# Unused tiles of 64 and 192 bytes between the pools of a fused linear-attention and gated-MLP kernel

## The chip, the core and the metric

The kernel runs on one core of a Trainium2 chip. The core has five engines that matter here: PE (TensorE, matrix products), DVE (VectorE), ACT (ScalarE), POOL (GpSimd) and SP (which here only issues DMAs). In the profile, PEld is the loading of a matmul's stationary operand, PE the streaming of the moving operand through it. The metric is the device time of one execution in microseconds (us), lower being better: before the change the median of three runs is 1317.28 us (1316.2 to 1317.75).

## What is computed

Everything is float32. Linear attention over 8 batches, 8 heads, 576 positions and head size 64, then a gated MLP on 4608 tokens of width 512 with a hidden width of 1536:

```python
def phi(x):
    proj = np.einsum('bhsd,df->bhsf', x, w_phi)
    proj = proj - np.max(np.abs(proj), axis=-1, keepdims=True)
    return np.concatenate([np.exp(proj), np.exp(-proj)], axis=-1)
q_p, k_p = (phi(q), phi(k))
kv = np.einsum('bhsf,bhsd->bhfd', k_p, v)
z = np.sum(k_p, axis=2)
attn = einsum('bhsf,bhfd->bhsd', q_p, kv) / (einsum('bhsf,bhf->bhs', q_p, z)[..., None] + 1e-06)
x = attn.transpose(0, 2, 1, 3).reshape(4608, 512)
xn = x / sqrt(mean(x * x, axis=-1) + 1e-06) * rms_g
g, val = xn @ w_gate, xn @ w_val
return (g / (1 + exp(-g)) * val) @ w_out
```

## The kernel before

**Products in three matmuls.** Most operands are split into a high and a low part of the type fp32r (`_split`, L59 to L61: ACT copies the high part, DVE or POOL subtracts to get the low one). A product is then three matmuls, high by high, high by low, low by high, added up in PSUM. Each matmul has a stationary operand of 128 columns, loaded anew every time, and a moving operand of 65 to 512 columns.

**Stages.** The program has three stages, written one after the other, with some overlap.

*Attention with fill.* 32 pairs of heads go through a software pipeline (`front`, `mid`, `back`, `last`), in which the parts of several pairs are merged by hand-given due times. Between them stand pieces of two other kinds: weights arrive in 64-bit form and are decoded, and *fill* units compute the first 3 of the 12 columns of blocks (128 wide) of `w_gate` and `w_val` for 256 tokens at a time, as soon as their x is complete. `fill` (L468) splits x into the tile `xo` of the pool `a_xf` (two buffers) and each unit issues 12 matmuls (L482): the weight `fg` or `fv` is stationary, `xo` moves, 256 columns wide. ACT copies the result to `fo`, also of pool `a_xf`, six buffers (L485), and a DMA stores it. When the last pair is done, the units that are left run one after the other.

*Gate.* For nine blocks of 512 tokens the other 9 columns of blocks are computed (`gv`, L602). `parts` (L168) puts x's high and low part into the tile `xb` of pool `xo0` for even blocks and of pool `xo1` for odd ones. Each product has 12 matmuls at L614: the weight (`fg`, `fv`, or `wg`, `wv` of the pools `m_w0` to `m_w5`) is stationary, `xb` moves, 512 columns wide. A block has 18 such products, 216 matmuls. While it runs, the next block's x is fetched, normalised and split. Silu and product go to DRAM as `h`.

*Out.* For 18 groups of 256 tokens `h` is read back and multiplied by `w_out` by a Strassen-like scheme of 7 products (`omm`, L785). Each has 6 weight places `kp` (0 to 5) and three matmuls for each place, in the order high weight, low weight, high weight (L789 and L790): here the operand from x (`a11h` and its like) is stationary and the weight (`wh`, `wl`) moves, 256 columns wide. So a product has 18 matmuls and a group 126. Places 0 to 3 come from pool `rg`, which lies at the right end of the memory; places 4 and 5 from the pools `owp4` and `owp5` on the left.

```python
for i, (a, w) in enumerate(((xh, wh), (xh, wl), (xl, wh))):
    nc.tensor.matmul(place[n], a[:, kp], w[:, o], start=(first and kp == 0 and i == 0),
```

**Addresses.** A pool takes its bytes per partition off a stack when it is opened; the pools of one stage stand in the order in which they are opened, and a stage's stack lies over that of the stage before. Tiles begin at multiples of 32 bytes. In this layout the operands of the matmuls start at these bytes of each partition; the offsets of their slices are multiples of 512, so that the remainder mod 256 holds for each matmul of a row:

| stage | moving operand: bytes, mod 256 | stationary operand: bytes, mod 256 |
|---|---|---|
| projections (L319 to L321) | `wh`, `wl` 143392, 144416: 32 | `th`, `tl` 100832 to 106976: 224 |
| fill | `xo` 60192, 68384: 32 | `fg`, `fv` 21280 to 39712: 32 |
| gate, odd blocks | `xb` of `xo1` 68384: 32 | `fg`, `fv` and `wg`, `wv` 84768 to 148256: 32 |
| gate, even blocks | `xb` of `xo0` 101152: 32 | the same: 32 |
| out, places 0 to 3 | `wh`, `wl` 163808 to 213984: 224 | x's operands 52000 to 106272: 32 |
| out, places 4 and 5 | `wh`, `wl` 82720, 89888, 117536, 124704: 32 | the same: 32 |

**Who waits for bytes.** A pool that lands on bytes of released pools waits in one of two ways. With `reuse_waits="tile"` each tile waits only for the users of the earlier tiles on its own bytes; gate's and out's pools have this. Without it all tiles of the pool wait for every user of the pools that it lands on.

**Order.** Each engine executes its instructions in the order of the program; all large DMAs but those of x's 256-token loads and the gate weights stand in SP's queue.

Of the kernel before, what the change touches and what calls it, by code (L numbers as in the profile page):

```python
# [8 lines left out]
F32 = mybir.dt.float32  # L9
# [73 lines left out]
def kernel(ctx: ExitStack, tc: tile.TileContext, q, k, v, w_phi,  # L83
# [108 lines left out]
        waiting.update(i.name for i in nc.cur_bb.bb.instructions[n:])  # L192


    a_ctx = ExitStack()
    xfp = a_ctx.enter_context(tc.tile_pool(name="a_xf", bufs=2))
    ndp = a_ctx.enter_context(tc.tile_pool(name="a_nd", bufs=2))
    xips.append(a_ctx.enter_context(tc.tile_pool(name="a_xi", bufs=1)))
    wk = a_ctx.enter_context(tc.tile_pool(name="a_wk", bufs=2))
# [3 lines left out]
    dec = a_ctx.enter_context(tc.tile_pool(name="a_dec", bufs=1))  # L203
# [357 lines left out]
    g_ctx = ExitStack()  # L561
# [4 lines left out]
    def own(name, bufs=1):  # L566
        return g_ctx.enter_context(tc.tile_pool(name=name, bufs=bufs, reuse_waits="tile"))

    dec, xo1 = own("m_dec"), own("xo1")
    wps = {j: own(f"m_w{j}") for j in (4, 5)}  # L570
    xops = [own("xo0"), xo1]
    wps.update((j, own(f"m_w{j}")) for j in range(4))
    wk = own("m_wk", 2)
    pg_ctx = ExitStack()
# [123 lines left out]
    def left(name, bufs=1):  # L698
        return ctx.enter_context(tc.tile_pool(name=name, bufs=bufs, reuse_waits="tile"))

    ohp, stp, xof = left("ohp", 2), left("stp", 2), left("xof")
    owps = [left("owp4")]
    xol, osp = left("xol"), left("osp", 8)
    owps.append(left("owp5"))
    ow = left("ow", 3)
    opools = dict(a22=xol, s4=xol)
    ps_g = ctx.enter_context(tc.tile_pool(name="ps_g", bufs=2, reuse_waits="tile", space=PSUM))
# [66 lines left out]
    for gi in range(NG):  # L774
# [8 lines left out]
        ro = ow.tile([128, 5, DH], F32, name="ro")  # L783
# [78 lines left out]
```

## Time and profile before

| | |
|---|---|
| median of three runs | 1317.28 us |
| the profiled execution's own time | 1319.19 us |
| its span, first to last instruction | 1315.7 us |
| mean granted TensorE clock in it | 0.995 |
| instructions | 24224 |
| matmuls of gate (L614), of fill (L482), of out (L790) | 1944, 1296, 2268 |
| bytes moved by DMA | 197.12 MB |

The span is shorter than the execution by 3.5 us, the launch and the end. Busy times and starts are read from one profiled execution, in us from the start of the span. The ends of matmuls are modelled, so that two matmuls overlap in it; the interval from one start to the next is what tells the pace, and that is what is read below. The chain of work that ended last is followed back from the last instruction; where PE stands on it without a break, the pace of its matmuls is the pace of the kernel.

### The profile page before, as it was taken

The numbers are of one execution on the slowest core, as the hardware profiler recorded it, in microseconds if no ns is written. First come the engines' busy times: TensorE is split into PE (matmuls) and PEld (weight loads), VectorE is DVE, ScalarE is ACT, GpSimd is POOL, SyncE is SP. The second block draws the span as 40 slices with busy tenths as digits, with TensorE's granted clock in tenths as the row PEclk, the third lists the DMA queues.
The fourth block names the chain that finished last, engine by engine and source line by source line (L and its number), as shares of the span: only waits on it lengthen the run. The fifth ranks groups of instructions, "written<-read, shape, count | busy, mean of one in ns | idle before, by whom it ended". The sixth has DMA issues, their size and how long they took to land.

```text
span 1315.7 us, 24224 instructions
## 1 busy us (share of the span) xinstructions
PE 1279.0 (97%) x8886; PEld 1190.3 (90%) x8886; DVE 839.8 (64%) x1228; ACT 705.3 (54%) x1472; POOL 623.7 (47%) x580
## 2 busy tenths in 40 slices
PE   7989999999999999899999999999999999999998
PEld 7989989999999898899888888888888899999998
DVE  7889887787788962311245645644545786788773
ACT  6878787787778874534233433432332444444442
POOL 4666665565555854201323223323211277776773
PEclk9999999999999999999999999999999999999999
DMA  5445575666656437444536435434425544445441
GB/s 163 127 128 149 163 183 144 156 182 170 172 160 177 126 102 214 159 153 138 170 102 210 144 130 198 145 126 162 139 87 165 185 142 148 144 131 164 143 141 48
DMA packets 198228, 197.12 MB, mean 150 GB/s; under 512 B 69024, under 2 KB 154912, under 8 KB 198112
## 3 DMA queue, kind: packets, MB, share of 16 engines
q1 hardware_dynamic: 179104, 181.44, 45.1%
q10 hardware_dynamic: 19008, 14.16, 4.0%
q8 instruction: 70, 1.15, 0.4%
q14 instruction: 46, 0.38, 0.1%
HBM read 126.04 MB, written 69.50 MB: 149 GB/s over the span
## 4 chain that ended last, share of the span: by engine, by line
PE 85%; DVE 5%; DMA 5%; ACT 2%; issue 1%; SPq 1%; POOL 0%; ACTq 0%; POOLq 0%; DVEq 0%
PE gp L614 18%; PE gq L614 15%; PE gd L790 6%; PE gy L790 6%; PE gz L790 6%; PE sm L482 6%; PE acc L359 6%; PE fp L482 5%; PE sm L423 4%; PE fp L790 3%; PE fp L423 2%; PE pp L321 2%; PE pp L319 2%; PE pp L320 2%; PE sm L372 2%; PE sm L306 2%
## 5 line engine op out<-in xcount | busy, mean ns | idle before, releaser
L388 POOL TENSOR_TENSOR ql<-eq,qh 128x256 fp32r<-128x256 f32 x256 | 216.8, 879 | 58.6 <-issue 31.7
L599 DVE TENSOR_TENSOR h<-sl,gp 128x512 f32<-128x512 f32 x81 | 55.5, 685 | 167.4 <-PE gp L614 153.5
L614 PE MATMUL gp<-xb,wv 128*128 128x512 f32 x648 | 158.4, 389 | 0.0
L614 PEld LDWEIGHTS gp<-xb,wv 128*128 128x128 f32 x648 | 121.2, 188 | 24.7
L614 PE MATMUL gq<-xb,wg 128*128 128x512 f32 x576 | 138.3, 389 | 0.0
L54 POOL TENSOR_TENSOR wa<-raw,wa 128x192 f32<-128x192 f32 (+1 forms) x112 | 66.8, 618 | 140.2 <-DVE wa L52 46.1
L359 PE MATMUL acc<-vm,ek 128*128 128x65 f32 x1024 | 131.0, 270 | 0.0
L614 PEld LDWEIGHTS gq<-xb,wg 128*128 128x128 f32 x576 | 108.1, 188 | 22.4
L359 PEld LDWEIGHTS acc<-vm,ek 128*128 128x128 f32 x1024 | 127.4, 194 | 0.5 <-ACT ek L346 0.4
L323 DVE TENSOR_REDUCE mx<-pp 128x4 f32<-128x512 f32 (+1 forms) x160 | 100.9, 631 | 30.4 <-PE pp L321 29.0
L384 ACT ACTIVATE qh<-sm 128x512 fp32r<-128x512 f32 (+1 forms) x192 | 97.4, 508 | 0.0
L597 ACT ACTIVATE sl<-gq 128x512 f32<-128x512 f32 x72 | 42.7, 593 | 97.0 <-PE gq L614 94.7
L319 PE MATMUL pp<-wh,th 128*128 128x256 f32 x288 | 88.6, 309 | 4.7 <-ACT th L60 1.5
L61 POOL TENSOR_TENSOR xb<-x,xb 128x1024 fp32r<-128x1024 f32 x18 | 46.3, 2594 | 97.9 <-ACT xb L60 97.9
L383 ACT ACTIVATE eq<-sm 128x512 f32<-128x512 f32 x128 | 78.5, 613 | 14.2 <-PE sm L372 11.1
L321 PE MATMUL pp<-wh,tl 128*128 128x256 f32 x288 | 84.4, 299 | 0.2 <-DVE tl L61 0.2
L320 PE MATMUL pp<-wl,th 128*128 128x256 f32 x288 | 81.2, 283 | 0.0
L614 PE MATMUL gp<-xb,fv 128*128 128x512 f32 x324 | 77.8, 389 | 0.0
L346 ACT ACTIVATE ek<-yk 128x512 f32<-128x512 f32 x128 | 75.3, 649 | 1.1 <-DVE yk L326 1.1
L154 POOL TENSOR_TENSOR ss<-ss,sq 128x512 f32<-128x512 f32 x27 | 34.9, 1291 | 80.9 <-ACT sq L153 80.9
L614 PEld LDWEIGHTS gp<-xb,fv 128*128 128x128 f32 x324 | 60.8, 188 | 12.6
L614 PE MATMUL gq<-xb,fg 128*128 128x512 f32 x288 | 69.2, 389 | 0.0
(210 smaller groups left out, 3803.4 us busy)
## 6 DMA issues: line engine op xcount, KB each, us to landing
hs<-h SPq DMA_DIRECT2D x108, 256.0 KB
ht<-hs SPq DMA_DIRECT2D x18, 1536.0 KB
gvs<-fo SPq DMA_DIRECT2D x108, 128.0 KB
gvr<-gvs SPq DMA_DIRECT2D x27, 512.0 KB
rc<-di SPq DMA_DIRECT2D x32, 288.0 KB
x<-xs ACTq DMA_DIRECT2D x18, 512.0 KB
x<-xs SPq DMA_DIRECT2D x9, 1024.0 KB
kt<-in_k_dram SPq DMA_DIRECT2D x32, 256.0 KB
```

The costliest lines, as they stand in the source:

```text
L319: nc.tensor.matmul(o, th[:, cs], wh, start=True, stop=False)
L320: nc.tensor.matmul(o, th[:, cs], wl, start=False, stop=False)
L321: nc.tensor.matmul(o, tl[:, cs], wh, start=False, stop=True)
L323: nc.vector.tensor_reduce(mx[:, 0:2 * m], pp[:, 0:2 * m], axis=AX.X, op=ALU.max, apply_absolute_value=True)
L359: nc.tensor.matmul(acc[:, sg, h], e[h][:, sg, j], vm[:, h, j], start=False, stop=(h == 1 and j == T0 - 1))
L383: nc.scalar.activation(ei[:, sg], yi, AF.Exp, scale=1.0 - 2.0 * sg)
L384: nc.scalar.activation(hi[:, sg], yi, AF.Exp, scale=1.0 - 2.0 * sg)
L388: nc.gpsimd.tensor_tensor(lo[:, sg, cs], ei[:, sg, cs], hi[:, sg, cs].bitcast(F32), ALU.subtract)
L423: nc.tensor.matmul(o[:, 0:SH], a[:, h, sg], e[:, sg, h, cs], start=(i == 0), stop=(i == 5))
L482: nc.tensor.matmul(fp[:, 0:TF], w, xx[x][:, c], start=(i == 0), stop=(i == 3 * NC - 1))
L614: nc.tensor.matmul(gp[:, 0:T], w, e[:, c], start=(i == 0), stop=(i == 3 * NC - 1))
L790: nc.tensor.matmul(place[n], a[:, kp], w[:, o], start=(first and kp == 0 and i == 0), stop=(kp == KP - 1 and i == 2), skip_group_check=True)
```

## The change

The change adds a function that opens a pool with one tile of n bytes per partition, which nothing writes or reads, and calls it ten times. In the attention stage it stands ahead of the pool of `xo` and `fo` (192 bytes) and behind it (64). In gate it stands around `xo1` (192 ahead, 64 behind) and around `xo0` (64 ahead, 192 behind). In out it stands around `owp4` and around `owp5` (192 ahead, 64 behind each). No instruction of the program is added, removed or moved by it in the source; the new pools are opened without `reuse_waits`.

```diff
+    def pad(c, at, n):
+        c.enter_context(tc.tile_pool(name=f"pad{at}", bufs=1)).tile([128, n // 4], F32, name=f"pad{at}")
+
     a_ctx = ExitStack()
+    pad(a_ctx, "x", 192)
     xfp = a_ctx.enter_context(tc.tile_pool(name="a_xf", bufs=2))
+    pad(a_ctx, "n", 64)
     ndp = a_ctx.enter_context(tc.tile_pool(name="a_nd", bufs=2))
...
-    dec, xo1 = own("m_dec"), own("xo1")
+    dec = own("m_dec")
+    pad(g_ctx, "xo1", 192)
+    xo1 = own("xo1")
+    pad(g_ctx, "w4", 64)
     wps = {j: own(f"m_w{j}") for j in (4, 5)}
+    pad(g_ctx, "xo0", 64)
     xops = [own("xo0"), xo1]
+    pad(g_ctx, "w0", 192)
     wps.update((j, own(f"m_w{j}")) for j in range(4))
...
     ohp, stp, xof = left("ohp", 2), left("stp", 2), left("xof")
+    pad(ctx, "ow4", 192)
     owps = [left("owp4")]
+    pad(ctx, "xol", 64)
     xol, osp = left("xol"), left("osp", 8)
+    pad(ctx, "ow5", 192)
     owps.append(left("owp5"))
+    pad(ctx, "ro", 64)
     ow = left("ow", 3)
```

Added up along each stack, the remainders become these; all other operands keep theirs, since each pair of tiles adds up to 256 bytes:

| operand | mod 256 before | after | moving less stationary, before | after |
|---|---|---|---|---|
| `xo` (fill, moving), and `fo` | 32 | 224 | 0 | 192 |
| `xb` of `xo1` (gate, odd blocks, moving) | 32 | 224 | 0 | 192 |
| `xb` of `xo0` (gate, even blocks, moving) | 32 | 96 | 0 | 64 |
| `wh`, `wl` of `owp4` and `owp5` (out, moving) | 32 | 224 | 0 | 192 |

## The prediction

> **What bounds the kernel now.** First the page's busy times, then the windows (each engine's busy time in a stretch; the first column of numbers is the stretch's length), then the chain of waits, then single instructions.
>
> ```profile
> PE 1279.0 (97%) x8886; PEld 1190.3 (90%) x8886; DVE 839.8 (64%) x1228; ACT 705.3 (54%) x1472; POOL 623.7 (47%) x580
> PE 85%; DVE 5%; DMA 5%; ACT 2%; issue 1%; SPq 1%; POOL 0%; ACTq 0%; POOLq 0%; DVEq 0%
> ```
> ```profile
> 200.00:300.00 100.00, 96.97 (x806) 95.61 (x805) 80.78 (x146) 80.57 (x202) 59.28 (x74) 0.98 0.60 165
> 300.00:400.00 100.00, 99.80 (x850) 99.41 (x849) 80.15 (x138) 76.85 (x196) 55.29 (x68) 1.00 0.59 161
> 500.00:554.00 54.00, 47.30 (x299) 42.63 (x298) 14.51 (x17) 22.05 (x44) 17.93 (x13) 0.97 0.63 195
> 554.00:630.00 76.00, 76.00 (x614) 74.97 (x613) 14.87 (x20) 30.66 (x73) 8.74 (x7) 1.00 0.45 144
> 680.00:730.00 50.00, 50.00 (x222) 41.44 (x221) 26.57 (x40) 19.28 (x33) 14.69 (x16) 1.00 0.49 163
> 1100.00:1200.00 100.00, 100.00 (x868) 100.00 (x867) 74.58 (x68) 42.03 (x55) 77.20 (x35) 1.00 0.48 146
> ```
>
> PE is the bound: from 554 us on it never stops, while DVE, ACT and POOL have room. Up to 500 us it is at 95 to 99%; only from 500 to 554 us it stops for 6.7 us. So what counts is the interval between the starts of two matmuls. The chain gives it (start, length, what, number):
>
> ```profile
> 579.87 8.62 PE sm L482 x72
> ...
> 772.16 2.72 PE gp L614 x12
> ...
> 1051.28 4.17 PE gy L790 x36
> ...
> 1065.84 2.20 PE gy L790 x19
> ```
>
> Gate: 2.72 us for 12, 226.7 ns each, 512 columns wide. Fill: 8.62 us for 72, 119.7 ns, 256 wide. A column thus costs (226.7 - 119.7) / 256 = 0.418 ns, 107 ns for 256 and 214 ns for 512, and both kinds pay some 13 ns for each matmul on top, whatever its width. Out: a group takes 1065.84 - 1051.28 = 14.56 us for 126, 115.6 ns each, also 256 wide: 4 ns less than fill, for a matmul of one form. The timeline of out says where that comes from (start, length, line, names):
>
> ```profile
> 1065.68 0.28 PE L790 MATMUL gy<-wh,a12h 128*128 128x256 f32 x1
> ...
> 1066.03 0.28 PE L790 MATMUL gy<-wh,a12h 128*128 128x256 f32 x1
> ...
> 1067.05 0.28 PE L790 MATMUL gy<-wh,a12h 128*128 128x256 f32 x1
> ...
> 1067.76 0.28 PE L790 MATMUL gy<-wh,s2h 128*128 128x256 f32 x1
> ```
>
> These are the starts of weight places 0, 1 and 4, and of the next product. Places 1 to 3 take (1067.05 - 1066.03) / 9 = 113.3 ns each, 6 above the columns; places 4 and 5 take 0.71 / 6 = 118.3 ns; place 0, the first after 4 and 5 of the product before, takes 0.35 / 3 = 116.7 ns. Line, width, type and stationary operand are the same; what differs is the weight's place in memory, 224 mod 256 against an operand at 32 for places 0 to 3, and 32 against 32 for 4 and 5. Fill and gate have 32 against 32 throughout, and pay the 13 ns throughout. This pair of paces is the heart of the forecast: equal remainders cost some 7 ns for each matmul, a distance of 192 does not.
>
> A third distance occurs in the projections, moving `wh` at 32, stationary `th` at 224, so a distance of 64 (of 256):
>
> ```profile
> 279.90 0.28 PE L319 MATMUL pp<-wh,th 128*128 128x256 f32 x1
> ...
> 280.84 0.28 PE L321 MATMUL pp<-wh,tl 128*128 128x256 f32 x1
> ```
> ```profile
> 25.76 0.28 PE L319 MATMUL pp<-wh,th 128*128 128x256 f32 x1
> ...
> 27.01 0.28 PE L321 MATMUL pp<-wh,tl 128*128 128x256 f32 x1
> ```
>
> The first row of matmuls has nine, (280.84 - 279.90) / 8 = 117.5 ns, so 10.5 ns above the columns; the second has twelve, 1.25 / 11 = 113.6 ns. The distance of 64 has two paces, then, and I see no more than which instructions stand around it.
>
> **The change part by part.** The tiles issue nothing, so the whole effect is the pace at new addresses.
>
> *Out.* Places 4 and 5 go from distance 0 to 192, as places 1 to 3 have it. At 113.3 ns for all, a group takes 14.28 us instead of 14.56, 0.28 us less, times 18 groups: 5.0 us. I take **4.9**. All rows are of this line itself; the cover is that nothing else is due within it. The nearest to it is the loop of `ht`: DVE's first work on a group waits for its load, and the next load is issued behind that work.
>
> ```profile
> 1107.36 1.59 DVE L726 TENSOR_TENSOR st<-ht 128x768 f32<-128x768 f32 x1 [3.35 <-DMA ht<-hs]
> ```
> ```profile
> 1120.81 0.96 DVE L726 TENSOR_TENSOR st<-ht 128x768 f32<-128x768 f32 x1 [2.23 <-DMA ht<-hs]
> ```
>
> It turned once in 13.45 us here, 0.8 us under the new 14.28. If it were the bound, the group could not go below it, and the change would still get its 0.28 us.
>
> *Fill.* The windows of L482 alone (busy time of PE and PEld, with counts):
>
> ```profile
> 450.00:500.00 50.00, 21.55 (x160) 20.06 (x161) 1.00 0.35 104
> 500.00:554.00 54.00, 28.60 (x214) 27.50 (x212) 0.97 0.63 195
> 554.00:630.00 76.00, 71.72 (x588) 71.53 (x588) 1.00 0.45 144
> ```
>
> Distance 0 becomes 192, at the same width as in out: 119.7 to 113.3 ns, 6.4 ns. From 554 us on, 588 matmuls give **3.8** us, since PE never stops there. The other 708 of the 1296 would give 4.5 us if PE set the end all the time; at 95 to 99% busy with chains of small DMAs between (DMA has 5% of the chain) I take 60%, **2.7** us, with 0 and 4.5 as ends. The `fo` tiles shift with `xo`: their stores move the same bytes, and DMA is at 0.45 of its time from 554 us on; cost nothing, and with six buffers ACT would have to be late by units of 1.4 us before PE saw it.
>
> *Gate, odd blocks.* Distance 0 to 192, 4 blocks of 216 matmuls. No row shows 512 columns at another distance than 0. The ends: nothing, if the 13 ns of this width are no matter of addresses, and all 13 ns (11.2 us), if no cost were left. I take the row of out, 113.3 against 119.7 ns and the same 13 ns on top of the columns in gate and in fill: 6.4 ns, 864 x 6.4 = **5.5** us.
>
> *Gate, even blocks.* Distance 64, 5 x 216 = 1080 matmuls. By the nine matmuls of the projections (10.5 ns instead of 13) it is 2.5 ns, 2.7 us; by the twelve 6.4 ns, 6.9 us; nothing is the lower end. I take the nine, **2.6** us, because they stand in the steady part of the attention stage and the twelve at its first pairs. Nothing else becomes due: the next block's x is ready early.
>
> ```profile
> 739.35 4.83 POOL L61 TENSOR_TENSOR xb<-x,xb 128x1024 fp32r<-128x1024 f32 x2 [12.86 <-ACT xb L60]
> ```
> ```profile
> 1048.99 0.28 PE L790 MATMUL fp<-wh,a11h 128*128 128x256 f32 x1
> ```
>
> POOL has the parts of a block ready at 744.2 us. Out's first matmul starts at 1048.99; a block is 216 matmuls and, but for the last, two more of the same width for the next block's norm, 49.4 us, the last 49.0. Counted back from 1048.99, a block begins at 1048.99 - 49.0 - 5 x 49.4 = 753 us: 8.8 us of room, against some 1.4 us by which a block becomes shorter.
>
> Sum: 4.9 + 3.8 + 2.7 + 5.5 + 2.6 = 19.5 us. The profiled execution took 1319.2 us, so 1299.7; on the median of the runs shown, 1317.3, it makes **1297.8**.
>
> **The rivals.**
>
> *B, the distance of 64 is as good as 192.* For it: the twelve at 113.6 ns; gate is one long stream of one kind, and the pace of a stream seems to settle into one of two. Against it: the nine, also a stream, stay at 117.5. Time: 1080 x 3.9 ns = 4.2 us more, **1293.6**.
>
> *C, the 512-wide matmuls do not follow.* Their 13 ns could belong to the width or to what follows a matmul; all rows of gate have one pace, whatever the weight, so no row speaks for addresses there. Against it: the same 13 ns in fill, on another width. Then 8.1 us are lost: **1305.9**.
>
> *D, the addresses do nothing.* The difference between places could come from where the pools lie at large (places 0 to 3 lie above 163808, the others below 131872). Against it: the weights of gate are spread from 21280 to 150304 and show one pace. Then the time stays at **1317**. The Trainium skill's page "SBUF — State Buffer", section "Who interferes with whom", speaks for this case: it gives TensorE two read ports, one for the moving operand and one for the weight load, calls them independent, and has it that PE never waits on anyone. By that rule a load and a stream could not meet at any address. The trace disagrees in the 5 ns between the places of out.
>
> *E, slower: the new pools make the gate stage wait.* They are opened without `reuse_waits="tile"`, on bytes of the attention stage. If the wait for all users went over to what lies beside them, no gate unit could start before the last fill unit, at 630 us. Of L614 alone:
>
> ```profile
> 500.00:554.00 54.00, 19.86 (x83) 15.32 (x84) 0.97 0.63 195
> ```
>
> These 83 matmuls (83 x 226.7 ns = 18.8 us) fill gaps now and would come on top, and with them the first weights' way to PE, among it x's own split (4.83 us on POOL in the row above): some 24 us against 19.5 gained, **1322**. It decides as soon as the wait costs more than 19.5 us. Against it: nothing reads or writes the new tiles, so nothing of theirs could wait.
>
> **How the numbers follow.** The forecast, with 117.5 ns at the distance of 64, has 0.46, B 0.32, C 0.12, D 0.06, E 0.04. The forecast's own range, with 0 to 4.5 us from the fill units before 554 us, is 1296 to 1300.5, B's 1292 to 1296.5; a gate that loses all 13 ns on odd blocks would reach 1288. These two cases hold 0.78, so the range goes on to C: 1289 to 1306. Differences under 0.2% (2.6 us) can't be told from none by a measurement of this kernel. Forecast, B and C are faster by more than that, 0.90 together; D is the same, 0.06; E is slower, 0.04.
>
> **What would show it.** In the chain and timeline after: out's places 4 and 5 at 113.3 ns, and place 0 too, a group in 14.28 us; fill's 72 matmuls in 8.16 us instead of 8.62; gate's 12 matmuls in 2.64 us for odd blocks, and for even ones 2.69 (forecast) or 2.64 (B); 2.72 in both is C. With all three at their old pace it is D. L614 with no matmul before the last of L482 is E. The forecast is wrong, too, if PE begins to show idle time after 554 us, in out first behind the load of `ht`.

## The result, and the profile after

The changed kernel is slower. Its median over 10 runs is 1325.16 us (1319.94 to 1328.27); the kernel before, run beside it, has 1314.72 us over 10 runs (1311.03 to 1317.75). The ratio is 1.0075, with a 95% interval of 1.0056 to 1.0094. The forecast was 1297.8 us and the range ended at 1306. The profiled execution took 1327.44 us, its span is 1324.4 us.

First the page of the kernel after: the busy times, and the chain's share of each engine.

```profile
PE 1285.8 (97%) x8886; PEld 1188.9 (90%) x8886; DVE 843.5 (64%) x1228; ACT 704.9 (53%) x1472; POOL 624.8 (47%) x580
...
PE 81%; DVE 8%; DMA 4%; ACT 3%; issue 2%; SPq 1%; POOL 1%; ACTq 0%; POOLq 0%; DVEq 0%
```

The counts are those of before and PE is busy 6.8 us longer. The windows show that it still never stops from 554 us on (length of the stretch, then busy time and count of PE, PEld, DVE, ACT and POOL):

```profile
554.00:630.00 76.00, 76.00 (x617) 74.21 (x616) 14.47 (x22) 30.88 (x73) 10.27 (x8) 1.00 0.48 151
...
1100.00:1200.00 100.00, 100.00 (x851) 100.00 (x850) 75.07 (x68) 41.51 (x55) 73.57 (x35) 1.00 0.49 148
```

The two lines point in opposite directions: 617 matmuls where there were 614 in the first stretch, 851 where there were 868 in the second. No wait was added; the pace itself changed, for the better in one stage and for the worse in another. The chain of waits of the kernel after gives the paces (start, length, what, how many):

```profile
567.85 8.48 PE sm L487 x72
...
576.80 8.17 PE sm L487 x72
...
625.38 24.73 PE gp L624 x108
...
790.58 2.80 PE gq L624 x12
...
812.77 2.75 PE gq L624 x12
...
1054.97 4.24 PE gy L804 x36
...
1069.81 4.24 PE gy L804 x36
...
1307.25 4.24 PE gy L804 x36
```

- Fill (L487): 8.48 / 72 = 117.8 ns in one row, 8.17 / 72 = 113.5 ns in the next. Before it was 119.7. So fill gains, but one row keeps a worse pace than the next at the same addresses.
- Gate (L624): odd blocks 2.80 / 12 = 233.3 ns, even blocks 2.75 / 12 = 229.2 ns. Before, both took 226.7. Gate loses in every block.
- Out (L804): a group takes 1069.81 - 1054.97 = 14.84 us instead of 14.56.

For the sums of the stages two more rows of the chain of before are needed, the start of gate and the last row of the first product:

```profile
629.79 24.51 PE gp L614 x108
...
1298.80 4.16 PE gy L790 x36
```

| stretch | before | after | difference |
|---|---|---|---|
| up to the start of gate's long row | 629.79 | 625.38 | -4.4 |
| from there to the first whole `gy` row of out | 421.49 | 429.59 | +8.1 |
| 17 groups of out | 247.52 | 252.28 | +4.8 |

Together +8.5 us, of the 8.7 us by which the spans differ. In out the single matmuls show what happened to the pair of paces that was the heart of the forecast; these are again places 0, 1 and 4 and the next product, in the timeline of the kernel after:

```profile
1069.65 0.28 PE L804 MATMUL gy<-wh,a12h 128*128 128x256 f32 x1
...
1070.00 0.28 PE L804 MATMUL gy<-wh,a12h 128*128 128x256 f32 x1
...
1071.06 0.28 PE L804 MATMUL gy<-wh,a12h 128*128 128x256 f32 x1
...
1071.77 0.28 PE L804 MATMUL gy<-wh,s2h 128*128 128x256 f32 x1
```

Places 1 to 3 take 1.06 / 9 = 117.8 ns, places 4 and 5 take 0.71 / 6 = 118.3 ns, the same within the 10 ns to which the rows are given. The moved places did not come to 113.3. The places that nobody moved left it: same tiles, same addresses as before, and 4.5 ns more for each matmul. So a matmul's pace isn't a property of its own two addresses alone.

### The profile page after: what moved, and what is told of

Same layout as the page of the kernel before. It is cut to its first block, busy times and chain, and to the rows that moved or that the text cites. A ratio compares the mean times of both kernels' runs of the same rounds, so it can differ in the third digit from the quotient of the medians.

```text
span 1324.4 us, 24224 instructions
## 1 busy us (share of the span) xinstructions
PE 1285.8 (97%) x8886; PEld 1188.9 (90%) x8886; DVE 843.5 (64%) x1228; ACT 704.9 (53%) x1472; POOL 624.8 (47%) x580
## 4 chain that ended last, share of the span: by engine, by line
PE 81%; DVE 8%; DMA 4%; ACT 3%; issue 2%; SPq 1%; POOL 1%; ACTq 0%; POOLq 0%; DVEq 0%
PE gp L624 18%; PE gq L624 15%; PE gd L804 6%; PE gz L804 6%; PE gy L804 6%; PE sm L487 5%; PE acc L364 5%; PE fp L487 4%; PE sm L428 4%; PE fp L804 3%; PE pp L326 2%; PE fp L428 2%; PE pp L324 2%; PE pp L325 2%; DVE mx L328 1%
## 5 line engine op out<-in xcount | busy, mean ns | idle before, releaser
L624 PE MATMUL gp<-xb,wv 128*128 128x512 f32 x648 | 161.2, 394 | 0.0
L624 PEld LDWEIGHTS gp<-xb,wv 128*128 128x128 f32 x648 | 121.2, 188 | 27.4 <-ACT sl L607 0.2
L624 PE MATMUL gq<-xb,wg 128*128 128x512 f32 x576 | 140.9, 393 | 0.0
L624 PEld LDWEIGHTS gq<-xb,wg 128*128 128x128 f32 x576 | 108.2, 188 | 25.0
L624 PE MATMUL gp<-xb,fv 128*128 128x512 f32 x324 | 79.2, 393 | 0.0
L624 PEld LDWEIGHTS gp<-xb,fv 128*128 128x128 f32 x324 | 60.9, 188 | 13.9
L624 PE MATMUL gq<-xb,fg 128*128 128x512 f32 x288 | 70.5, 393 | 0.0
```

The source lines that it names most:

```text
L624: nc.tensor.matmul(gp[:, 0:T], w, e[:, c], start=(i == 0), stop=(i == 3 * NC - 1))
```

## The experiments

Two questions stood open after the result. Why did out's unmoved places lose 113.3 ns? And do 512-wide matmuls follow the same rule as 256-wide ones? The theories: **L**, that a row of matmuls at distance 192 (moving less stationary, mod 256) has two steady paces, some 113.3 and 117.8 ns, and keeps the one that its beginning leads it into; and its rivals, that it is the **alignment** of the two starts within 64 bytes that counts, not their distance; that out took over its pace from the changed **gate**; and that each place keeps its own pace, so that the loss came from somewhere else.

**A map of paces.** This kernel computes nothing of the reference. It runs rows of 30 fp32r matmuls on constant data, 256 or 512 wide, with the stationary operand at 32 or at 0 mod 256 and the moving one at ten distances, behind none, one or two short matmuls.

```diff
+SETS = [(256, 32, [0, 16, 32, 64, 96, 128, 160, 192, 224, 240]), (256, 0, [...]), (512, 32, [...]), (512, 0, [...])]
+            nc.tensor.matmul(p[:, 0:width], wt[:, s0 + (i % 12) * 128:s0 + (i % 12 + 1) * 128],
+                             xt[:, m0 + (i // 3 % 4) * width:m0 + (i // 3 % 4 + 1) * width], start=(i == 0), stop=(i == n - 1))
```

> This kernel computes nothing of the reference: it runs streams of 30 fp32r matmuls on constant data, 256 and 512 columns wide, with the stationary operand at 32 or 0 mod 256 and the moving one at a distance of 0, 16, 32, 64, 96, 128, 160, 192, 224 or 240 bytes from it, each three times, behind nothing, one or two short matmuls. Theory P (each pair of remainders has one pace): each distance has one interval in all three streams, about 113 ns (256 wide) at 64 and 192, about 120 at 0. Theory L (a stream at another distance than 0 has two steady paces and keeps the one into which its beginning leads it): at 64 and 192 some streams of 256 columns hold 113.3 ns and others 117.7 from their first ten matmuls to the end, at 0 all hold 120; at 512 columns 0 gives 226.7 and the others 229 or 233, or a faster pace near 220. Theory A (the 6.7 ns that remain at 113.3 come from starting at 32 within 64 bytes): the streams with both operands at a multiple of 64 are faster than 113.3 and 220 ns.

The timeline shows each row of 30 in one line. The name of its tile holds width, remainder of the stationary operand, distance and the number of short matmuls ahead (p256s32d64r0). From the start of one row to that of the next is the time of 30 matmuls:

```profile
21.59 3.56 PE L110 MATMUL p256s32d64r0x<-xt,wt 128*128 128x256 f32 x30
24.99 3.76 PE L110 MATMUL p256s32d96r0x<-xt,wt 128*128 128x256 f32 x30
28.59 3.73 PE L110 MATMUL p256s32d128r0x<-xt,wt 128*128 128x256 f32 x30
...
442.26 7.00 PE L110 MATMUL p512s0d0r0x<-xt,wt 128*128 128x512 f32 x30
449.10 7.11 PE L110 MATMUL p512s0d16r0x<-xt,wt 128*128 128x512 f32 x30
```

At 256 wide, distance 64 takes (24.99 - 21.59) / 30 = 113.3 ns and 96 takes 3.60 / 30 = 120.0 ns. At 512 wide, distance 0 takes 6.84 / 30 = 228.0 ns, with the beginning of the row in it. Taking the last 18 intervals of each row alone, and both remainders of the stationary operand:

| distance | 256 wide, ns | 512 wide, ns |
|---|---|---|
| 0 | 120.0 | 226.7 |
| 64 | 113.3 in one row, 117.8 in the two behind short matmuls | 228.9 |
| 192 | 113.3; with the stationary at 0: 113.3 once, 117.8 twice | 233.3 |
| 96 | 120.0 | 233.3 |
| 16 to 240, the others | 116.4 to 120.0 | 231.3 to 236.7 |

Three things follow. At 256 wide distance 0 is among the worst, as the forecast had it. At 512 wide it is the best. And at 64 and 192 the same row of matmuls can have 113.3 or 117.8 ns, depending on what went ahead. Alignment falls: with the stationary operand at 0 or at 32 the values are the same but for which of two paces is met. Nor are 64 and 192 alone in this: 240 has 233.3 or 236.7 ns at 512 wide, 16 has 116.7 or 118.7 ns at 256 wide, by what went ahead.

The map also answers what the forecast took for granted. 226.7 ns is twice 113.3: at the best pace of each width a column costs 0.443 ns, and no fixed cost for each matmul shows on top. The 13 ns that the forecast found on top of the columns came of comparing the best pace at 512 with one of the worst at 256.

**Out alone.** Only the four tiles around `owp4` and `owp5`.

```diff
+    pad(ctx, "ow4", 192)
     owps = [left("owp4")]
+    pad(ctx, "xol", 64)
...
+    pad(ctx, "ow5", 192)
     owps.append(left("owp5"))
+    pad(ctx, "ro", 64)
```

> Only the four unused tiles of the out stage are left, fill and gate stand as before. Theory P: places 0 to 5 all at 113.3 ns, a group of 126 in 14.28 us instead of 14.56, some 5 us faster. Theory L: without the matmuls at distance 0 in places 4 and 5, which lead the stream back to 113.3 ns in each product, the whole stage holds one pace, as in the changed kernel 117.7 ns: a group in 14.84 us, 5 us slower. If the pace of out in the changed kernel was carried over from its gate stage, out is at 113.3 here and the kernel 5 us faster.

It took 1322.34 us over 6 runs beside 1316.08 for the kernel before, ratio 1.0042 (1.0021 to 1.0063). Its chain:

```profile
588.04 8.62 PE sm L485 x72
...
1050.36 4.24 PE gy L797 x36
1065.19 4.24 PE gy L797 x36
```

Fill keeps its old 8.62 us for 72. The group takes 14.83 us, as in the full change, and all six places stand between 117.7 and 118.0 ns. Gate is untouched here, so the worse pace isn't carried over from gate: taking the three matmuls of each of places 4 and 5 away from distance 0 is enough to lock the whole stage at 117.8 ns.

**Fill alone.** Only the 192 bytes ahead of `a_xf` and the 64 behind.

```diff
+    pad(a_ctx, "x", 192)
     xfp = a_ctx.enter_context(tc.tile_pool(name="a_xf", bufs=2))
+    pad(a_ctx, "n", 64)
```

> Only the two unused tiles around the pool of x's parts in fill are left, gate and out stand as before. Both theories expect a gain from fill alone. Theory P: all 72 matmuls of a block at 113.3 ns, 8.16 us instead of 8.62, some 6 us faster in all. Theory L: some streams at 113.3 and some at 117.7 ns, 8.16 or 8.48 us, some 4 us faster, with gate at 2.72 us for 12 and out at 14.56 for a group as before.

1310.40 us over 4 runs, ratio 0.9955 (0.9938 to 0.9973): this part is a gain. Its chain:

```profile
571.92 8.48 PE sm L487 x72
...
1042.46 4.17 PE gy L795 x36
1057.02 4.16 PE gy L795 x36
```

Out's group stays at 14.56 us. Five rows of 72 in the stage's end all take 8.48 us, 117.8 ns: here fill met only the worse of the two paces, and still gained 1.9 ns on 119.7.

**A finer map.** The same rows at 32 distances in steps of 8, two rows each, stationary at 32; it too computes nothing of the reference.

```diff
-SETS = [(256, 32, [0, 16, 32, 64, ...
+SETS = [(512, 32, [0, 8, 16, 24, ..., 248]), (256, 32, [0, 8, 16, 24, ..., 248])]
```

> As the first map (nothing of the reference is computed), with the distance in steps of 8 bytes from 0 to 248, 512 and 256 columns, two streams each. Theory M (the steady pace is a function of width and distance, with two steady paces at 64 and 192 for 256 columns): the values of the first map come again at its distances, 226.7 ns at 0, 228.9 at 64 and 233.3 at 192 for 512 columns, and no distance between is under 226.7. A rival: there is a distance at which 512 columns run near 220 ns, which the coarse map stepped over; then gate could be made faster by shifting x's parts there.

```profile
11.55 6.99 PE L110 MATMUL p512s32d0r0x<-xt,wt 128*128 128x512 f32 x30
18.38 7.17 PE L110 MATMUL p512s32d8r0x<-xt,wt 128*128 128x512 f32 x30
...
179.04 7.16 PE L110 MATMUL p512s32d192r0x<-xt,wt 128*128 128x512 f32 x30
186.04 7.14 PE L110 MATMUL p512s32d200r0x<-xt,wt 128*128 128x512 f32 x30
...
490.79 3.69 PE L110 MATMUL p256s32d64r0x<-xt,wt 128*128 128x256 f32 x30
494.32 3.75 PE L110 MATMUL p256s32d72r0x<-xt,wt 128*128 128x256 f32 x30
...
512.31 3.61 PE L110 MATMUL p256s32d112r0x<-xt,wt 128*128 128x256 f32 x30
515.76 3.81 PE L110 MATMUL p256s32d120r0x<-xt,wt 128*128 128x256 f32 x30
```

512 wide: 6.83 us at distance 0, 7.00 us at 192; in the last 18 intervals 226.7 ns at 0 is the lowest of all 32, 228.9 at 64 the next, the highest 236.7. 256 wide: distance 64 now takes 3.53 / 30 = 117.7 ns behind a row at 56, where the first map had 113.3 for the same pair of addresses behind a row at 32. That is theory L in one pair of lines. Distance 112 came to 113.3 ns both times, and 120 is the worst with 122.2.

**Gate alone.** Only the four tiles around `xo1` and `xo0`.

```diff
+    pad(g_ctx, "xo1", 192)
+    xo1 = own("xo1")
+    pad(g_ctx, "w4", 64)
     wps = {j: own(f"m_w{j}") for j in (4, 5)}
+    pad(g_ctx, "xo0", 64)
     xops = [own("xo0"), xo1]
+    pad(g_ctx, "w0", 192)
```

> Only the four unused tiles around xo1 and xo0 in gate are left. Theory M: 12 matmuls take 2.80 us in odd blocks (192) and 2.75 in even ones (64), as the first map has it for 512 columns, against 2.72: 864 x 6.7 + 1080 x 2.2 ns = 8 us slower, and fill and out as before. Theory P, on which the prediction was built: 2.64 us in odd blocks, 5 us faster or more.

1324.69 us over 9 runs beside 1316.45, ratio 1.0059 (1.0032 to 1.0087).

```profile
668.09 2.80 PE gq L622 x12
...
718.72 2.75 PE gq L622 x12
...
763.28 2.80 PE gq L622 x12
```

The blocks alternate at 233.3 and 229.2 ns, the values of the maps at distances 192 and 64. From the last fill matmul to out's first it is 428.0 us, 8.5 more than the 419.5 before. By the maps one expects 864 x 6.6 ns + 1080 x 2.2 ns = 8.1 us. The three parts alone make +6.3, -5.7 and +8.2 us, together +8.8; the whole change made +10.4.

**Fill with place 4 alone, fill with place 5 alone.** If the three matmuls at distance 0 are what leads the others back to 113.3 ns, one place left at 0 must do.

```diff
+    pad(a_ctx, "x", 192)
     xfp = a_ctx.enter_context(tc.tile_pool(name="a_xf", bufs=2))
+    pad(a_ctx, "n", 64)
...
+    pad(ctx, "ow4", 192)
     owps = [left("owp4")]
+    pad(ctx, "xol", 64)
```

The second kernel has the same two tiles in fill, and in out these:

```diff
+    pad(ctx, "ow5", 192)
     owps.append(left("owp5"))
+    pad(ctx, "ro", 64)
```

> The tiles of fill, and in out those around place 4 alone; place 5 stays at distance 0. Theory L: the three matmuls of place 5 lead the stream back to 113.3 ns in each product, so places 1 to 4 hold about 113.3, and only 5 and 0 are slower: a group in about 14.4 us instead of 14.56, 3 us faster than with fill's tiles alone (1310.4). If it takes more matmuls at distance 0 to lead it back, the stage holds 117.8 ns, 14.84 us, and the kernel is 5 us slower than with fill's tiles alone.

> The tiles of fill, and in out those around place 5 alone; place 4 stays at distance 0. Theory L: as with place 4 alone: either places 5 and 0 to 3 hold about 113.3 ns and a group takes about 14.4 us, or the stage holds 117.8 and a group takes 14.8 us. Which of the two places is the better one no theory says.

The chain of the first:

```profile
1043.87 4.13 PE gy L797 x36
1058.30 4.12 PE gy L797 x36
```

The group takes 14.42 us, under the 14.56 of before. In the median of the products, places 1 to 4 run at 113.3 ns, place 4 among them, now that it is at 192; place 5, at 0, has 116.0 and place 0 behind it 117.3. In the second kernel it is the same one place on: places 0 to 3 have 113.3 ns, place 4, at 0, has 116.0 and place 5 behind it 117.3. The first kernel took 1308.93 us (10 runs, ratio 0.9957, 0.9935 to 0.9979), the second 1312.29 us (10 runs, 0.9971, 0.995 to 0.9992), and out is 260.4 us long in both, 2.4 less than before (first to last matmul). The 3.4 us between their medians can't be put down to out. In the profiles the long row of gate starts at 622 us in the first and at 629.5 us in the second with equal paces of fill: the attention stage's end scatters by several us between executions.

The granted TensorE clock goes with this scatter. In the first profile it is 1.00 from 0 to 100 and from 200 to 300 us, in the second 0.97 and 0.98. Among 24 executions of the kernel before, the one at a mean of 0.991 took 1322.1 us and the two at 0.999 took 1311.1 and 1311.5. The ten executions of the first kernel have 0.996 on average, those of the second 0.995. A straight line with one slope through all of these (an estimate: some 1.45 us less for each 0.001 more) leaves the first 4.9 and the second 5.0 us under the kernel before at equal clock: the two are alike. What lowers the clock, and whether a change of addresses has a part in it, no run shows.

**Distance 112 in fill and in all of out.** By the finer map 112 has the good pace without choice. `xo` begins 16 bytes further inside a wider tile; in out, x's operands go to 112 and places 4 and 5 to 224, so that all of out is at 112.

```diff
+    pad(a_ctx, "x", 96)
...
-        xhl = xfp.tile([128, 2, NC, TF], F32R, name="xo")
+        xhl = xfp.tile([128, 2 * NC * TF + 64], F32R, name="xo")[:, 4:4 + 2 * NC * TF].rearrange("p (a c t) -> p a c t", a=2, c=NC)
...
+    pad(ctx, "xof", 64)
+    xof = left("xof")
+    pad(ctx, "ow4", 128)
     owps = [left("owp4")]
...
-            h, l = (opools.get(n, xof).tile(part, F32R, name=n + i) for i in "hl")
+            h, l = (opools.get(n, xof).tile([128, KP * 128 + 64], F32R, name=n + i)[:, 4:4 + KP * 128].rearrange("p (k c) -> p k c", k=KP) for i in "hl")
```

> Gate stays at distance 0, the best of 32 distances for 512 columns in the fine map. Fill and all places of out stand at a distance of 112 bytes, the one at which both 256-wide streams of the fine map came to 113.3 ns. Theory M: out at 113.3 to 114 ns in all places, a group in 14.3 us instead of 14.56 (5 us), and all fill streams at 113.3 (6 to 8 us): 11 to 13 us faster than before, near 1304. Rival: the pace at 112 needs the map's one long stream; with a new group every 12 or 18 matmuls the streams do not come to it (in the map its first eight intervals were 115 to 120 ns), and the gain is half of that or less.

1327.26 us over 8 runs, ratio 1.0073 (1.0048 to 1.0098).

```profile
534.11 49.28 PE sm L487 x432
...
1048.69 4.32 PE gy L803 x36
1063.82 4.32 PE gy L803 x36
```

Fill does as the map says: 49.28 / 432 = 114.1 ns. Out does not: 15.13 us for a group is 120 ns a matmul, as bad as distance 0 throughout. Fill has 144 against 32, out 224 against 112, and both differ by 112. So the distance doesn't say all either. Whether it is the new start of the stationary operand or the shorter rows of out that matter, this kernel doesn't separate.

The 10.8 us above the kernel before are not out's alone. Out is 10.0 us longer (272.88 against 262.85, first to last matmul). This kernel also has the stall of gate that the next section describes: from the last fill matmul to out's first it is 448.7 us instead of 419.5, and gate has no matmul from 500 to 554 us. Fill's gain lies against it.

**Fill at 112 with place 4.** Fill as in the last kernel, out as in the first of the pair.

```diff
+    pad(a_ctx, "x", 96)
     xfp = a_ctx.enter_context(tc.tile_pool(name="a_xf", bufs=2))
+    pad(a_ctx, "n", 160)
...
+        xhl = xfp.tile([128, 2 * NC * TF + 64], F32R, name="xo")[:, 4:4 + 2 * NC * TF].rearrange("p (a c t) -> p a c t", a=2, c=NC)
...
+    pad(ctx, "ow4", 192)
     owps = [left("owp4")]
+    pad(ctx, "xol", 64)
```

> Fill at a distance of 112, out as in the run with the tiles around place 4 alone (a group in 14.4 us). Theory M: fill at 113.3 ns throughout, so 3 to 4 us faster than that run in fill, and out 2.5 us under before: near 1306. If 112 does not hold in fill, the blocks of 72 matmuls take 8.3 us or more.

1316.52 us over 12 runs, ratio 0.9996 (0.9975 to 1.0017): no gain, with the best pace in fill and in out. The windows of L619 alone in this kernel (PE and PEld), and the chain:

```profile
500.00:554.00 54.00, 0.00 (x0) 0.00 (x0) 0.97 0.75 220
```

```profile
604.92 10.24 PE gp L619 x45
...
616.96 1.29 POOL ss L154
...
643.57 16.32 PE gp L619 x72
```

And the window after that wait (all of PE, then PEld, DVE, ACT, POOL; the third number from the end is the granted clock):

```profile
623.00:629.00 6.00, 6.00 (x14) 4.73 (x15) 0.00 (x0) 0.11 (x1) 1.24 (x1) 0.50 0.00 0
```

Gate has no matmul from 500 to 554 us, where it had 83. Its first one starts at 590.2 us instead of 496.7, only 15 of its matmuls come before the last of fill instead of 108, and PE waits there for ACT and POOL. The longest wait of the list of waits names the tile:

```profile
POOL xb L61 <- DMA gvs<-fo: 57.3, 1, 57.3
```

The wider tiles of `xo` moved the pools of the attention stage up by 768 bytes. By the layout `xo0` at 101152 then meets the last buffer of x's load, which ends at 101600, and a tile with `reuse_waits="tile"` waits for the users of its own bytes. From the last fill matmul to out's first it is 449.3 us instead of 419.5; 93 x 226.7 ns = 21.1 us of that are the matmuls that used to lie among fill. Most of the rest is PE: it starts nothing from 617.48 to 622.94 us, and from 623 to 629 us, at a granted clock of 0.50, its matmuls are 427 ns apart, 2.8 us more for 14. Out's 2.4 us and fill's gain were paid back here. That it is `xo0` and this overlap is read from the layout (the row of waits puts the end down to a store of `fo`); the next kernel tests whether the layout is the cause.

**The same with gate moved along.** One tile of 768 bytes ahead of gate's pools restores the overlaps.

```diff
+    pad(g_ctx, "g", 768)
     dec, xo1 = own("m_dec"), own("xo1")
```

> As the run with fill at 112 and the tiles around place 4, but all pools of gate stand 768 bytes higher, as far as the wider tiles of fill have moved the pools of the attention stage, so that xb of block 0 no longer lies on bytes of the last x load of fill. If the late start of gate in that run (448.7 us from the last fill matmul to the first of out instead of 419.5) came from that overlap, gate's first units run among the fill units again, 419.5 us, and the kernel is near 1306, 10 us under before. If it came from something else, it stays near 1316.

1309.18 us over 6 runs beside 1316.96, ratio 0.9944 (0.9927 to 0.9962).

```profile
562.91 8.21 PE sm L487 x72
...
1055.29 4.12 PE gy L798 x36
1069.71 4.12 PE gy L798 x36
```

From the last fill matmul to out's first it is 419.5 us again, fill has 8.21 / 72 = 114.0 ns and the group 14.42 us. So the layout was the cause of the stall (the 448.7 us of the expectation is the value of the kernel with 112 in all of out; the one it means had 449.3). Since all of gate's pools moved, which of the overlaps did it isn't separated. This kernel beats before and after; from fill alone (0.9955) and fill with place 4 (0.9957) its interval doesn't tell it apart.

**Place 5 at 112 too.** The last matmuls at distance 0 go to 112 (144 against 32), by a wider tile as in fill.

```diff
+        if kp == 5:
+            wh, wl = (pool.tile([128, 7 * DH + 64], F32R, name=f"w{c}{kp}")[:, 4:4 + 7 * DH].rearrange("p (o d) -> p o d", o=7) for c in "hl")
...
+    pad(ctx, "ow5", 96)
     owps.append(left("owp5"))
+    pad(ctx, "ro", 160)
```

> As the run beside it, with place 5 of out at 144 mod 256, a distance of 112 with the stationary operand still at 32, as in the fine map. If a mix of 192 and 112 keeps the pace of 113.3 ns, a group takes 14.3 us instead of 14.46 and the kernel is 3 us faster than the run beside it. If the three matmuls at distance 0 in place 5 are what leads places 0 to 4 to 113.3, these fall back to 117.7 ns, a group takes 14.8 us, and it is 6 us slower than the run beside it.

1315.31 us over 12 runs, ratio 0.9988 (0.997 to 1.0006), 6.1 us above the kernel of the last experiment.

```profile
1063.98 4.20 PE gy L803 x36
1078.68 4.20 PE gy L803 x36
```

The timeline shows where place 5 starts and where the next product does:

```profile
1080.24 0.29 PE L803 MATMUL gy<-wh,a12h 128*128 128x256 f32 x1
...
1080.62 0.28 PE L803 MATMUL gy<-wh,s2h 128*128 128x256 f32 x1
```

The group rises from 14.42 to 14.70 us: 0.28 us times 18 groups is 5.0, and out is 5.0 us longer (265.43 against 260.46). Place 5 takes 0.38 / 3 = 126.7 ns here, 125.3 in the median of the products, more than any distance had in the maps. Places 0 and 1 behind it have 118.0 and 116.7, and places 2 to 4 have 113.3. Neither branch of the expectation came. The three matmuls at distance 0 cost less than what came in their place; but places 2 to 4 keep the better pace with no matmul at distance 0 in the product, so it isn't distance 0 as such that leads them to it. That it is the change of distance within the row fits all of these kernels, and isn't tested further.

## Why the prediction was wrong

**The heart, "equal remainders cost some 7 ns for each matmul, a distance of 192 does not", failed.** It read 113.3 ns at places 1 to 3 as the pace of their addresses. It was the pace of a mixed row, in which each product has six matmuls at distance 0. With all places at 192 the same places run at 117.8 (out alone); with three matmuls of 18 left at 0 they run at 113.3 (fill with place 4). At distances 64 and 192 a 256-wide row has two paces, and something in its beginning selects. The sign of this stood in the forecast's own rows: the projections had 117.5 and 113.6 ns at one distance. It was used as two prices of the distance 64; it was a warning about 192.

**Out, -4.9 us forecast, +5.0 measured (267.85 against 262.85 us, first to last matmul).** 14.28 us for a group was expected, 14.84 came. The direction turned on the step above. That nothing else is due within the stage was right: PE has no idle time in it. Half of the gain can be had: moving place 4 alone gives 14.42 us a group and 2.4 us.

**Gate, odd blocks, -5.5 forecast, and even ones, -2.6; together +8.1 measured.** The step that failed is the carrying over from 256 to 512 columns, "the same 13 ns on top of the columns in gate and in fill". Those 13 ns were drawn from two rows, one of each width, both at distance 0, as if a matmul had a fixed cost there; by the maps gate had nothing on top to lose. At 512 wide distance 0 is the best of 32 distances with 226.7 ns; 64 costs 2 ns more and 192 costs 6.6 ns more. The forecast said that no row shows 512 columns at another distance and then took "nothing" as the lower end, without a reason that excludes a loss. With an end as far below nothing as above, the range would have held slower times. (In the even term 2.5 ns is the 13 less 10.5; with the 12.7 that the rows give it is 2.2 ns, 2.4 us. That changes nothing here.)

**Fill, -3.8 and -2.7: right in sign, too large.** 8.16 us for 72 was expected; 8.48 and 8.17 came in turn, and 8.48 throughout in fill alone. At 117.8 ns the 588 matmuls from 554 us on gain 588 x 1.9 = 1.1 us. Before 554 us the intervals between fill's matmuls (those under 140 ns) are 119.4 ns on average in the kernel before and 116.1 in fill alone, so the 708 there gain at most 708 x 3.3 = 2.3 us. The three kernels with fill at 192 and gate as before were 5.7, 7.5 and 4.2 us under the kernel before in their medians; without the 2.4 us of out in the last two that leaves 5.7, 5.1 and 1.8 us for fill. Much of the spread is the granted clock: at equal clock, by straight lines as above, it is some 3.8, 2.5 and 2.6 us (estimates, to 2.4 us either way in the first, 1.5 in the others), as much as the paces allow. The forecast's reading that PE is at 95 to 99% up to 500 us doesn't hold at the start (87% from 0 to 100 us); only 16 fill matmuls lie before 200 us, so the sum doesn't hang on it.

**The rivals.** B, 64 as good as 192, holds for 256 wide, where both have the same two paces, but not for gate, which it was about: there 64 is the better by some 4 ns and both are worse than 0. C, that the 512-wide matmuls don't follow, was the nearest, but it had them at no change; they follow in the other direction. D, that addresses do nothing, is refuted by the maps: 113.3 to 122.2 ns at 256 wide, 226.7 to 236.7 at 512 wide. The Trainium skill's page "SBUF — State Buffer", section "Who interferes with whom", calls PE's two read ports independent and has PE never wait on anyone; spreads of 8% and 4% with the two addresses are not what that rule would give, though no run shows what waits for what. E didn't happen: in the profile after, gate has 78 matmuls from 500 to 554 us where it had 83. Its kind of mechanism appeared where it wasn't looked for, with fill's wider tiles.

**What stays open.** Why there are two paces, and what in the beginning of a row selects one, wasn't found. Nor why 144 against 32 and 224 against 112 differ, nor why 144 against 32 holds 113.3 to 114.1 ns in the map and in fill but costs 125 in place 5 of out. What lowers the granted clock in some executions is open too. The last 2 us between the sum of the parts and the whole change lie within the intervals.

## What to carry to other kernels

A pace read from a mixed row of matmuls is a property of the row: before all of it is made like its best part, try that alone, for each width. Where no row shows an operation in its new state, a loss is as possible as a gain until something excludes it. A shift of a few hundred bytes in a stacked layout also changes which released tiles lie below, so after each such edit look at whether the first units of the next stage still start where they did.

## What the runs showed of the hardware

- The interval between fp32r matmuls, each with its own weight load, depends on the two operands' starts mod 256 bytes: by 8% at 256 columns (113.3 to 122.2 ns) and 4% at 512 (226.7 to 236.7). The order of distances isn't the same for both widths: 0 is among the worst for one and the best for the other.
- Some distances (64, 192) have two steady paces at 256 columns, 113.3 and 117.8 ns, that can last for a whole stage: the changed kernel's out stayed at the worse one for 268 us, while its fill changed from one to the other between rows of 72.
- Three matmuls of 18 at distance 0 brought 12 of the other 15 to the better pace: 14.42 us for a group against 14.84 without them. Three at distance 112 brought 9 of 15 to it, but took 125 ns each: 14.70 us.
- In fill at 112 with place 4, PE started nothing for 5.5 us; in the 6 us behind it the granted clock was 0.50 and 512-wide matmuls were 427 ns apart instead of 226.7.
- The executions of one kernel differ with the mean granted clock: 1322.1 us at 0.991, 1311.1 and 1311.5 at 0.999 (kernel before).
